# A first layer by seven products for eight, and head pairs mixed with weight conversion, in an attention and gated-FFN kernel

One core of a Trainium2 chip. The metric is device time in microseconds (us), median of several runs; "faster" and "slower" mean by more than 2%.

## The reference

Linear attention without a softmax on 8 batches x 8 heads x 576 tokens x 64, an RMS norm per head, then a gated FFN on 4608 tokens; all float32, except that the three weight matrices arrive as float64.

```python
kv  = einsum('bhsd,bhse->bhde', k, v)
out = einsum('bhsd,bhde->bhse', q, kv)
x   = out / sqrt(mean(out * out, -1) + 1e-6) * g_norm      # (B,H,S,D) -> (B*S, H*D) = (4608, 512)
gate = 1 / (1 + exp(-(x @ w_gate)))                        # w_gate, w_val: (512, 1536)
return (gate * (x @ w_val)) @ w_out                        # w_out: (1536, 512)
```

## The kernel before

It works on nine chunks of 512 tokens. The first layer is one accumulation of four 128x128 by 128x512 matmuls for the gate and four for the value, for each of 12 tiles of 128 features. The weights come in as 64-bit words and are turned into float32 by bit operations, 36 tiles in all (24 for the first layer, then 12 `wo`): GpSimd and ScalarE limit the high word, VectorE does five instructions, GpSimd the last add. Attention of a batch is 16 steps (four for each of 4 head pairs), put one at a time between matmul groups of the chunk ahead. The code is shortened; `...` marks what is left out.

```python
def convert(u):                                  # one weight tile
    ...
    vec.scalar_tensor_tensor(out=yf, in0=a, scalar=HI_MIN, in1=xf, op0=ALU.is_ge, op1=ALU.mult)
    vec.tensor_scalar(out=z, in0=y, ..., op0=ALU.bitwise_and, op1=ALU.logical_shift_left)      # "first mask"
    vec.scalar_tensor_tensor(out=y, in0=y, scalar=0xC0000000, in1=z, ...)
    vec.tensor_scalar(out=z, in0=y, scalar1=0xFF800000, scalar2=None, op0=ALU.bitwise_and)
    vec.scalar_tensor_tensor(out=zf, in0=lo, scalar=2.0 ** -52, in1=zf, op0=ALU.mult, op1=ALU.mult)
    limit(u + 1)
    nc.gpsimd.tensor_tensor(out=flat, in0=zf, in1=yf, op=ALU.add)
    ...

def in_step(c, f):                               # first layer, chunk c, features f
    pg, pv = mm_ps(), mm_ps()
    for ps, name in ((pg, "wg"), (pv, "wv")):
        for m in range(NMT):                     # 4
            nc.tensor.matmul(ps, w[name, f][:, m, :], xT[c][:, m, :], start=(m == 0), stop=(m == NMT - 1))
    nc.scalar.activation(out=sg, in_=pg, func=AF.Sigmoid)
    nc.vector.tensor_tensor(out=gv[c, f], in0=pv, in1=sg, op=ALU.mult)

limit(0)
for step in attention(0): step()                 # batch 0 whole, then conversion begins
convert(0); convert(1)
...
for i, (c, step) in enumerate(todo):             # first layers of chunks 0 and 1, both second layers, then chunk by chunk
    ...
    if ahead: ahead.pop(0)()                     # one attention step of the next batch
    while done < min(2 * i + 4, 2 * NFT) or ...: # about two tiles to a feature step
        convert(done); done += 1
    step()
```

## Time and profile before

| | before |
|---|---|
| time, median (lowest to highest) | 1302.28 us (1301.61 to 1303.0) |
| profiled span | 1298.5 us |
| first attention ends / chunk 1 begins | 54.5 us / 182 us |
| steady chunk with attention / without | 137.2 us / 123.6 us |

The views behind these rows are shown in the prediction. Two more groups by shape matter later (columns: line, engine, operation, output from inputs, shapes, count, busy us, mean ns, idle us before and what ended it): the first mask of the conversion, and the transposes behind the normalising product.

```profile
L122 DVE TENSOR_SCALAR cz<-cy 128x512 uint32<-128x512 uint32 x36 | 27.8, 771 | 1.2
L216 PE MATMUL at<-ident,xn 96*128 96x96 f32 x192 | 23.3, 261 | 20.7 <-DVE xn L208 20.7
```

In the whole kernel TensorE waits 20.7 us for normalising products, all of it in the first attention and in the flush before 182 us (attention steps that are left over and run by themselves).

### The profile page before, as it was taken

The numbers are of one execution on the slowest core, as the hardware profiler recorded it, in microseconds if no ns is written. First come the engines' busy times: TensorE is split into PE (matmuls) and PEld (weight loads), VectorE is DVE, ScalarE is ACT, GpSimd is POOL, SyncE is SP. The second block draws the span as 40 slices with busy tenths as digits, with TensorE's granted clock in tenths as the row PEclk, the third lists the DMA queues.
The fourth block names the chain that finished last, engine by engine and source line by source line (L and its number), as shares of the span: only waits on it lengthen the run. The fifth ranks groups of instructions, "written<-read, shape, count | busy, mean of one in ns | idle before, by whom it ended". The sixth has DMA issues, their size and how long they took to land.

```text
span 1298.5 us, 10116 instructions
## 1 busy us (share of the span) xinstructions
PE 1242.4 (96%) x4128; PEld 599.2 (46%) x4128; DVE 292.8 (23%) x451; ACT 254.2 (20%) x417; POOL 108.1 (8%) x114
## 2 busy tenths in 40 slices
PE   4688879999999999999999999999999999999998
PEld 3443344444444544444444444444444444444443
DVE  1699955520001110111011101110111001000100
ACT  2323332321012211221122112211122110000000
POOL 1366623300000000000000000000000000000000
PEclk8699989999999999999999999999999999999999
DMA  8254423200021102111111011110200000000000
GB/s 188 76 153 138 133 78 117 77 18 25 24 63 28 28 17 62 28 28 26 44 46 28 18 43 37 29 27 24 63 1 1 25 9 0 1 24 9 1 8 25
DMA packets 62350, 57.29 MB, mean 44 GB/s; under 512 B 40800, under 2 KB 53088, under 8 KB 62304
## 3 DMA queue, kind: packets, MB, share of 16 engines
q1 hardware_dynamic: 56960, 37.76, 11.5%
q0 software_dynamic: 5184, 18.88, 4.5%
q8 instruction: 33, 0.54, 0.2%
q14 instruction: 13, 0.11, 0.0%
q10 hardware_dynamic: 160, 0.00, 0.0%
HBM read 47.19 MB, written 9.44 MB: 44 GB/s over the span
## 4 chain that ended last, share of the span: by engine, by line
PE 88%; DVE 8%; issue 1%; DMA 1%; ACT 1%; SPq 0%; POOL 0%; DVEq 0%; ACTq 0%
PE mm L244 52%; PE mm L264 29%; PE at L197 3%; DVE cy L123 2%; PE at L176 2%; DVE cz L122 2%; DVE cy L120 2%; PE at L216 1%; DVE cz L125 1%; PE at L187 1%; DMA v<-in_v_dram 1%; DVE xn L208 1%; DVE gv L248 1%; DVE ms L204 0%; DMA q<-in_q_dram 0%
## 5 line engine op out<-in xcount | busy, mean ns | idle before, releaser
L244 PE MATMUL mm<-xT,wg 128*128 128x512 f32 x864 | 395.5, 601 | 11.4 <-POOL wg L130 11.4
L244 PE MATMUL mm<-xT,wv 128*128 128x512 f32 x864 | 389.5, 593 | 5.9 <-POOL wv L130 5.9
L264 PE MATMUL mm<-wo,gv 128*128 128x512 f32 x864 | 375.4, 592 | 0.0
L244 PEld LDWEIGHTS mm<-xT,wv 128*128 128x128 f32 x864 | 163.2, 190 | 216.4 <-issue 197.8
L264 PEld LDWEIGHTS mm<-wo,gv 128*128 128x128 f32 x864 | 162.3, 190 | 195.2 <-issue 195.2
L244 PEld LDWEIGHTS mm<-xT,wg 128*128 128x128 f32 x864 | 158.4, 191 | 182.9 <-issue 167.7
L248 DVE TENSOR_TENSOR gv<-mm,sg 128x512 f32<-128x512 f32 x108 | 74.6, 691 | 611.2 <-PE mm L244 611.1
L246 ACT ACTIVATE sg<-mm 128x512 f32<-128x512 f32 x108 | 64.4, 596 | 352.2 <-PE mm L244 352.0
L266 ACT COPY out<-mm 128x512 f32<-128x512 f32 x36 | 21.1, 586 | 330.9 <-PE mm L264 275.2
L204 DVE TENSOR_REDUCE ms<-sq 96x12 f32<-96x768 f32 x32 | 30.3, 948 | 168.6 <-ACT sq L203 168.6
L197 PEld LDWEIGHTS at<-kv,qT 128*96 128x96 f32 x384 | 50.5, 180 | 14.6 <-issue 13.6
L197 PE MATMUL at<-kv,qT 128*96 128x128 f32 x384 | 53.2, 294 | 0.3 <-ACT xT L224 0.3
L180 DVE COPY kv<-at 64x64 f32<-64x64 f32 x64 | 14.2, 221 | 153.7 <-PE at L176 151.7
L203 ACT ACTIVATE sq<-at 96x768 f32<-96x768 f32 x32 | 25.8, 807 | 94.0 <-PE at L197 94.0
L224 ACT ACTIVATE xT<-at,g_col 128x288 f32<-128x288 f32 (+8 forms) x96 | 33.5, 421 | 54.5 <-PE at L216 54.5
L216 PE MATMUL at<-ident,xn 96*128 96x96 f32 x192 | 23.3, 261 | 20.7 <-DVE xn L208 20.7
L108 ACT ACTIVATE ca<-st 128x512 f32<-128x512 f32 x36 | 24.5, 680 | 94.6 <-DVE cy L120 46.3
L106 POOL TENSOR_SCALAR cx<-st 128x512 f32<-128x512 f32 x36 | 32.6, 906 | 95.6 <-DVE cy L120 88.7
L176 PEld LDWEIGHTS at<-v,k 96*64 96x64 f32 x768 | 27.6, 149 | 27.1 <-issue 24.7
L176 PE MATMUL at<-v,k 96*64 96x64 f32 x768 | 32.1, 238 | 6.3 <-DMA v<-in_v_dram 6.3
L123 DVE SCALAR_TENSOR_TENSOR cy<-cy,cz 128x512 uint32<-128x512 uint32 x36 | 37.1, 1031 | 1.2
L189 ACT COPY qT<-at 128x576 f32<-128x576 f32 x32 | 20.4, 638 | 86.4 <-PE at L187 86.4
(27 smaller groups left out, 350.1 us busy)
## 6 DMA issues: line engine op xcount, KB each, us to landing
k<-in_k_dram SPq DMA_DIRECT2D x32, 288.0 KB, 3.3
v<-in_v_dram SPq DMA_DIRECT2D x32, 288.0 KB, 3.8
q<-in_q_dram SPq DMA_DIRECT2D x64, 144.0 KB, 3.0
st<-in_moe_w_gate_dram POOLq DMA_DIRECT2D x12, 512.0 KB, 4.0
st<-in_moe_w_val_dram POOLq DMA_DIRECT2D x12, 512.0 KB, 4.3
st<-in_moe_w_out_dram POOLq DMA_DIRECT2D x12, 512.0 KB, 3.6
out_dram<-out SPq DMA_DIRECT2D x24, 192.0 KB, 2.3
out_dram<-out SPq DMA_DIRECT2D x24, 128.0 KB, 2.4
```

The lines of the kernel that those rows point to most:

```text
L106: nc.gpsimd.tensor_scalar(out=x.bitcast(FP32), in0=hi.bitcast(FP32), scalar1=HI_MAX, scalar2=-HI_MAX, op0=ALU.min, op1=ALU.max)
L120: vec.scalar_tensor_tensor(out=yf, in0=a, scalar=HI_MIN, in1=xf, op0=ALU.is_ge, op1=ALU.mult)
L123: vec.scalar_tensor_tensor(out=y, in0=y, scalar=0xC0000000, in1=z, op0=ALU.bitwise_and, op1=ALU.bitwise_or)
L176: nc.tensor.matmul(ps[HD * e:HD * e + HD, 0, 0:HD], kin[:, e, js], vin[:, e, js], start=(j == 0), stop=(j == NJ - 1))
L197: nc.tensor.matmul(ps[0:NP, j // JH, c0:c0 + P], qT[m][:, j // JH, NP * (j % JH):NP * (j % JH) + NP], kvs[m % 2], start=True, stop=True)
L204: nc.vector.tensor_reduce(out=ms.rearrange("p i n -> p (i n)"), in_=sq.rearrange("p i (n d) -> p (i n) d", d=HD), axis=AX.X, op=ALU.add)
L216: nc.tensor.transpose(ps[:, j // JH, c0:c0 + NP], xn[m][:, j // JH, P * (j % JH):P * (j % JH) + P], ident[0:NP, 0:NP])
L224: nc.scalar.activation(out=chunk(c)[:, m, o:o + n], in_=ps[:, i, r:r + n], func=AF.Copy, scale=g_col)
L244: nc.tensor.matmul(ps, w[name, f][:, m, :], xT[c][:, m, :], start=(m == 0), stop=(m == NMT - 1))
L246: nc.scalar.activation(out=sg, in_=pg, func=AF.Sigmoid)
L248: nc.vector.tensor_tensor(out=gv[c, f], in0=pv, in1=sg, op=ALU.mult)
L264: nc.tensor.matmul(ps, gv[c, f][:, P * t:P * t + P], w["wo", f], start=(f == 0), stop=(f == NFT - 1))
```

## The change

Its intent: fewer multiplications in the first layer, and a start in which conversion runs beside the first attention. For chunks 1 to 8 the two matrices (gate, value) and the two halves of the tokens and of the contraction form a 2x2 block product, done in Strassen's way (in the Winograd form) with seven products of 256 columns in place of eight. VectorE makes four sums of x per chunk, GpSimd four sums of weights per feature tile, and the products are added up as they leave the accumulators. Attention becomes 11 fine steps per head pair, taken one to a "slot" between products. Conversion becomes three stages per tile: 20 of the 108 stages go among the first attention, six go behind each feature of chunk 0, and the last 16 go one to a slot in the first half of chunk 1.

```diff
+    with tc.tile_pool(name="psum0", bufs=4, space=bass.MemoryType.PSUM) as psum0:
+        steps = [attention(n, ...) for n in range(NHP)]
+        for t in range(NHP + 2):
+            ...                                   # kv, q of pair t; x of pair t - 2
+            if 0 <= uu < NHP:
+                steps[uu][4](); steps[uu][5]()    # q x kv, square
+                convert_some(2)
+                steps[uu][6](); steps[uu][7]()    # sum, root
+            convert_some(2)
+            if 0 <= uu < NHP:
+                steps[uu][8]()                    # normalising product
...
+    def slot():
+        if fill: fill.popleft()()                 # one attention step
+        if slow: slow.popleft()()                 # one conversion stage (chunk 1, first half)
+    def first_layer(c):                           # chunk 0, plain
+        for f in range(NFT):
+            converted(2 * f + 1)
+            ... the eight matmuls, a slot() after each second one ...
+            nc.vector.tensor_tensor(out=gv_tile(c, f), in0=pv, in1=sg, op=ALU.mult)
+            convert_some(6)
...
+    def w_sum(f, i):                              # four per feature tile
+        nc.gpsimd.tensor_tensor(out=tw[f, i], in0=..., in1=..., op=ALU.subtract)      # 128x256
...
+            def product(ps, wt, xs, new):
+                for m in range(NK):               # 2
+                    nc.tensor.matmul(ps, wt[:, m, :], xs[:, m, :], ...)                # 256 columns
+            def p6():
+                product(pb, tw[f, 2], s[:, 1], True)
+                tt(out=d["h"][:, h1], in0=pb, in1=d["p1"], op=ALU.add)
+            ...                                   # p1, p2, p7, p5, p4, p3 likewise
+            def end(): tt(out=d["h"], in0=d["h"], in1=d["sg"], op=ALU.mult)
...
+    first_layer(0)
+    flush()
+    slow.extend(converts)
+    feed(2)
+    first_layer_fast(1, 0, NFT // 2)
+    while slow: slow.popleft()()
+    second_layer(0)
+    first_layer_fast(1, NFT // 2, NFT)
```

More of the change, by code (lines that the diff above doesn't have):

```diff
@@ L1 @@
 import struct
+from collections import deque
 from contextlib import ExitStack
@@ L43 @@
     NP = S // NJ
+    JH = NJ // 2
     NMT = DM // P
@@ L46, with load_kv @@
     G = 512
+    GH = G // 2
     NG = T // G
-    NLD = 2
     NST = 3
     const = ctx.enter_context(tc.tile_pool(name="const", bufs=1))
-    ld = ctx.enter_context(tc.tile_pool(name="ld", bufs=NLD))
     sb = ctx.enter_context(tc.tile_pool(name="sb", bufs=2))
-    psum = ctx.enter_context(tc.tile_pool(name="psum", bufs=2, space=bass.MemoryType.PSUM))
     ctx.enter_context(tc.manual_schedule())
     pairs = {}
-    def load_pair(n):
+    def load_kv(n):
         if n >= B * NHP:
@@ L63, in load_pair, with load_q @@
         b, h0 = n // NHP, 2 * (n % NHP)
-        pairs[n] = []
+        pairs[n] = {}
         for name, src in (("k", k), ("v", v)):
-            t = ld.tile([NP, 2, NJ * HD], FP32, tag=name, name=name)
+            t = sb.tile([NP, 2, NJ * HD], FP32, tag=name, name=name)
             nc.sync.dma_start(out=t, in_=src[b, h0:h0 + 2].rearrange("h (p j) d -> p h (j d)", j=NJ))
-            pairs[n].append(t)
-        t = ld.tile([NP, NJ, 2, HD], FP32, tag="q", name="q")
+            pairs[n][name] = t
+    def load_q(n):
+        if n >= B * NHP:
+            return
+        b, h0 = n // NHP, 2 * (n % NHP)
+        t = sb.tile([NP, NJ, 2, HD], FP32, tag="q", name="q")
         for e in range(2):
             nc.sync.dma_start(out=t[:, :, e, :], in_=q[b, h0 + e].rearrange("(p j) d -> p j d", j=NJ))
-        pairs[n].append(t)
+        pairs[n]["q"] = t
     units = []
@@ L102, in limit @@
         lo, hi = words(u)
-        x = sb.tile([P, UW], U32, tag="cx", name="cx", bufs=1)
-        a = sb.tile([P, UW], FP32, tag="ca", name="ca", bufs=1)
+        x = sb.tile([P, UW], U32, tag="cx", name="cx")
+        z = sb.tile([P, UW], U32, tag="cz", name="cz")
         nc.gpsimd.tensor_scalar(out=x.bitcast(FP32), in0=hi.bitcast(FP32), scalar1=HI_MAX, scalar2=-HI_MAX,
                                 op0=ALU.min, op1=ALU.max)
-        nc.scalar.activation(out=a, in_=hi.bitcast(FP32), func=AF.Abs)
@@ L109, in limit @@
-        ranged[u] = x, a
+        nc.scalar.activation(out=z.bitcast(FP32), in_=hi.bitcast(FP32), func=AF.Abs)
+        ranged[u] = x, z
     def convert(u):
         name, f, src, shape = units[u]
-        lo, hi = words(u)
-        x, a = ranged.pop(u)
-        y = sb.tile([P, UW], U32, tag="cy", name="cy")
-        z = sb.tile([P, UW], U32, tag="cz", name="cz")
-        xf, yf, zf = x.bitcast(FP32), y.bitcast(FP32), z.bitcast(FP32)
-        vec = nc.vector
-        vec.scalar_tensor_tensor(out=yf, in0=a, scalar=HI_MIN, in1=xf, op0=ALU.is_ge, op1=ALU.mult)
@@ L122, in convert @@
-        vec.tensor_scalar(out=z, in0=y, scalar1=0x07FFFFFF, scalar2=3, op0=ALU.bitwise_and, op1=ALU.logical_shift_left)
-        vec.scalar_tensor_tensor(out=y, in0=y, scalar=0xC0000000, in1=z, op0=ALU.bitwise_and, op1=ALU.bitwise_or)
-        vec.tensor_scalar(out=z, in0=y, scalar1=0xFF800000, scalar2=None, op0=ALU.bitwise_and)
-        vec.scalar_tensor_tensor(out=zf, in0=lo, scalar=2.0 ** -52, in1=zf, op0=ALU.mult, op1=ALU.mult)
-        limit(u + 1)
-        t = const.tile(shape, FP32, name=f"{name}{f}")
@@ L129, in convert, with fl, s0 @@
-        flat = t.rearrange("p m f -> p (m f)") if len(shape) == 3 else t
-        nc.gpsimd.tensor_tensor(out=flat, in0=zf, in1=yf, op=ALU.add)
-        w[name, f] = t
-        load_unit(u + NST)
-    load_pair(0)
-    for u in range(NST):
-        load_unit(u)
-    for n in range(1, NLD):
-        load_pair(n)
+        vec = nc.vector
+        def fl(t):
+            return t.bitcast(FP32)
+        def s0():
+            x, z = ranged[u]
+            vec.scalar_tensor_tensor(out=fl(x), in0=fl(z), scalar=HI_MIN, in1=fl(x), op0=ALU.is_ge, op1=ALU.mult)
@@ new lines, in s1, with s2 @@
+        def s1():
+            x, z = ranged[u]
+            vec.tensor_scalar(out=z, in0=x, scalar1=0x07FFFFFF, scalar2=3, op0=ALU.bitwise_and,
+                              op1=ALU.logical_shift_left)
+            vec.scalar_tensor_tensor(out=x, in0=x, scalar=0xC0000000, in1=z, op0=ALU.bitwise_and, op1=ALU.bitwise_or)
+        def s2():
+            x, z = ranged[u]
+            vec.tensor_scalar(out=z, in0=x, scalar1=0xFF800000, scalar2=None, op0=ALU.bitwise_and)
+            vec.scalar_tensor_tensor(out=fl(z), in0=words(u)[0], scalar=2.0 ** -52, in1=fl(z),
+                                     op0=ALU.mult, op1=ALU.mult)
+            limit(u + 1)
+            t = const.tile(shape, FP32, name=f"{name}{f}")
+            flat = t.rearrange("p m f -> p (m f)") if len(shape) == 3 else t
+            nc.gpsimd.tensor_tensor(out=flat, in0=fl(z), in1=fl(x), op=ALU.add)
+            w[name, f] = t
+            load_unit(u + NST)
@@ L141, with convert_some, converted @@
+        return [s0, s1, s2]
+    converts = deque(s for u in range(len(units)) for s in convert(u))
+    made = [0]
+    def convert_some(n):
+        for _ in range(min(n, len(converts))):
+            converts.popleft()()
+            made[0] += 1
+    def converted(u):
+        convert_some(3 * (u + 1) - made[0])
+    load_kv(0)
+    load_q(0)
+    load_unit(0)
+    load_kv(1)
+    load_q(1)
+    load_unit(1)
+    load_unit(2)
     ident = const.tile([P, P], FP32, name="ident")
@@ L159, in chunk, with attention, kv_mm @@
         return xT[c]
-    def at_ps():
-        return psum.tile([P, 2, 512], FP32, tag="at", name="at")
-    JH = NJ // 2
-    def attention(b):
-        qT, xn = {}, {}
-        def kv_step(m):
-            kin, vin, _ = pairs[NHP * b + m]
-            kv = kvs[m % 2]
-            ps = at_ps()
+    def attention(n, at_ps):
+        b, m = divmod(n, NHP)
+        d = {}
+        def kv_mm():
+            d["kv"] = ps = at_ps()
             for j in range(NJ):
@@ L175, in kv_step, with kv_out @@
                 for e in range(2):
-                    nc.tensor.matmul(ps[HD * e:HD * e + HD, 0, 0:HD], kin[:, e, js], vin[:, e, js],
+                    nc.tensor.matmul(ps[HD * e:HD * e + HD, 0, 0:HD], pairs[n]["k"][:, e, js], pairs[n]["v"][:, e, js],
                                      start=(j == 0), stop=(j == NJ - 1))
+        def kv_out():
             for e in range(2):
                 es = slice(HD * e, HD * e + HD)
-                nc.vector.tensor_copy(out=kv[es, es], in_=ps[es, 0, 0:HD])
@@ L182, in q_step, with q_mm @@
-        def q_step(m):
-            qin = pairs[NHP * b + m][2]
-            ps = at_ps()
+                nc.vector.tensor_copy(out=kvs[n % 2][es, es], in_=d["kv"][es, 0, 0:HD])
+            load_kv(n + 2)
+        def q_mm():
+            d["q"] = ps = at_ps()
             for j in range(NJ):
                 c0 = NP * (j % JH)
-                nc.tensor.transpose(ps[:, j // JH, c0:c0 + NP], qin[:, j].rearrange("p e d -> p (e d)"), ident[0:NP, 0:NP])
-            qT[m] = sb.tile([P, 2, JH * NP], FP32, tag="qT", name="qT")
-            nc.scalar.copy(out=qT[m], in_=ps[:, :, 0:JH * NP])
-            load_pair(NHP * b + m + NLD)
@@ L192, in u_step, with q_out, u_mm @@
-        def u_step(m):
+                nc.tensor.transpose(ps[:, j // JH, c0:c0 + NP], pairs[n]["q"][:, j].rearrange("p e d -> p (e d)"),
+                                    ident[0:NP, 0:NP])
+        def q_out():
+            d["qT"] = sb.tile([P, 2, JH * NP], FP32, tag="qT", name="qT")
+            nc.scalar.copy(out=d["qT"], in_=d["q"][:, :, 0:JH * NP])
+            load_q(n + 2)
+        def u_mm():
             ps = at_ps()
+            d["u"] = ps[0:NP, :, 0:JH * P]
             for j in range(NJ):
@@ L196, in u_step @@
                 c0 = P * (j % JH)
-                nc.tensor.matmul(ps[0:NP, j // JH, c0:c0 + P], qT[m][:, j // JH, NP * (j % JH):NP * (j % JH) + NP],
-                                 kvs[m % 2], start=True, stop=True)
-            u = ps[0:NP, :, 0:JH * P]
-            sq = sb.tile([NP, 2, JH * P], FP32, tag="sq", name="sq", bufs=1)
-            ms = sb.tile([NP, 2, 2 * JH], FP32, tag="ms", name="ms")
-            xn[m] = sb.tile([NP, 2, JH * P], FP32, tag="xn", name="xn", bufs=1)
-            nc.scalar.activation(out=sq, in_=u, func=AF.Square)
@@ L204, in u_step @@
-            nc.vector.tensor_reduce(out=ms.rearrange("p i n -> p (i n)"),
-                                    in_=sq.rearrange("p i (n d) -> p (i n) d", d=HD), axis=AX.X, op=ALU.add)
-            nc.scalar.activation(out=ms, in_=ms, func=AF.Sqrt, bias=eps[0:NP], scale=1.0 / HD)
-            nc.vector.reciprocal(ms, ms)
-            nc.vector.tensor_tensor(out=xn[m].rearrange("p i (n d) -> p i n d", d=HD),
-                                    in0=u.rearrange("p i (n d) -> p i n d", d=HD),
-                                    in1=ms.unsqueeze(3).to_broadcast([NP, 2, 2 * JH, HD]), op=ALU.mult)
@@ L212, in x_step, with u_square, u_sum @@
-        def x_step(m):
-            ps = at_ps()
+                nc.tensor.matmul(ps[0:NP, j // JH, c0:c0 + P], d["qT"][:, j // JH, NP * (j % JH):NP * (j % JH) + NP],
+                                 kvs[n % 2], start=True, stop=True)
+        def u_square():
+            d["sq"] = sb.tile([NP, 2, JH * P], FP32, tag="sq", name="sq", bufs=1)
+            nc.scalar.activation(out=d["sq"], in_=d["u"], func=AF.Square)
+        def u_sum():
+            d["ms"] = sb.tile([NP, 2, 2 * JH], FP32, tag="ms", name="ms")
+            nc.vector.tensor_reduce(out=d["ms"].rearrange("p i n -> p (i n)"),
+                                    in_=d["sq"].rearrange("p i (n d) -> p (i n) d", d=HD), axis=AX.X, op=ALU.add)
@@ new lines, in u_root, with u_norm @@
+        def u_root():
+            nc.scalar.activation(out=d["ms"], in_=d["ms"], func=AF.Sqrt, bias=eps[0:NP], scale=1.0 / HD)
+        def u_norm():
+            nc.vector.reciprocal(d["ms"], d["ms"])
+            d["xn"] = d["sq"]
+            nc.vector.tensor_tensor(out=d["xn"].rearrange("p i (n d) -> p i n d", d=HD),
+                                    in0=d["u"].rearrange("p i (n d) -> p i n d", d=HD),
+                                    in1=d["ms"].unsqueeze(3).to_broadcast([NP, 2, 2 * JH, HD]), op=ALU.mult)
@@ L214, in x_step, with x_mm, x_out @@
+        def x_mm():
+            d["x"] = ps = at_ps()
             for j in range(NJ):
                 c0 = NP * (j % JH)
-                nc.tensor.transpose(ps[:, j // JH, c0:c0 + NP], xn[m][:, j // JH, P * (j % JH):P * (j % JH) + P],
+                nc.tensor.transpose(ps[:, j // JH, c0:c0 + NP], d["xn"][:, j // JH, P * (j % JH):P * (j % JH) + P],
                                     ident[0:NP, 0:NP])
+        def x_out():
             s0 = 0
@@ L222, in x_step @@
                 i, r = divmod(s0, S // 2)
-                n = min(G - o, S // 2 - r)
-                nc.scalar.activation(out=chunk(c)[:, m, o:o + n], in_=ps[:, i, r:r + n], func=AF.Copy, scale=g_col)
-                s0 += n
-        steps = []
-        for t in range(NHP + 2):
-            for step, m in ((kv_step, t), (x_step, t - 2), (q_step, t), (u_step, t - 1)):
-                if 0 <= m < NHP:
-                    steps.append(lambda step=step, m=m: step(m))
-        return steps
-    gv = {}
@@ L237, in mm_ps @@
-    def mm_ps():
-        return psum.tile([P, 512], FP32, tag="mm", name="mm", bufs=4)
-    def in_step(c, f):
-        pg, pv = mm_ps(), mm_ps()
-        for ps, name in ((pg, "wg"), (pv, "wv")):
-            for m in range(NMT):
-                nc.tensor.matmul(ps, w[name, f][:, m, :], xT[c][:, m, :], start=(m == 0), stop=(m == NMT - 1))
-        sg = sb.tile([P, G], FP32, tag="sg", name="sg")
-        nc.scalar.activation(out=sg, in_=pg, func=AF.Sigmoid)
-        gv[c, f] = sb.tile([P, G], FP32, tag="gv", name="gv", bufs=2 * NFT)
-        nc.vector.tensor_tensor(out=gv[c, f], in0=pv, in1=sg, op=ALU.mult)
+                n_ = min(G - o, S // 2 - r)
@@ new lines, in x_out @@
+                nc.scalar.activation(out=chunk(c)[:, m, o:o + n_], in_=d["x"][:, i, r:r + n_], func=AF.Copy, scale=g_col)
+                s0 += n_
+        return [kv_mm, kv_out, q_mm, q_out, u_mm, u_square, u_sum, u_root, u_norm, x_mm, x_out]
+    limit(0)
+    with tc.tile_pool(name="psum0", bufs=4, space=bass.MemoryType.PSUM) as psum0:
+        steps = [attention(n, lambda: psum0.tile([P, 2, 512], FP32, tag="at", name="at")) for n in range(NHP)]
+        for t in range(NHP + 2):
+            kv, qq, uu, xx = t, t, t - 1, t - 2
+            if kv < NHP:
+                for i in range(4):
+                    steps[kv][i]()
+            if 0 <= xx < NHP:
+                steps[xx][9]()
+                steps[xx][10]()
+            if 0 <= uu < NHP:
+                steps[uu][4]()
+                steps[uu][5]()
+                convert_some(2)
+                steps[uu][6]()
+                steps[uu][7]()
+            convert_some(2)
+            if 0 <= uu < NHP:
+                steps[uu][8]()
@@ new lines, with feed, mm_ps @@
+    psum = ctx.enter_context(tc.tile_pool(name="psum", bufs=1, space=bass.MemoryType.PSUM))
+    fill = deque()
+    slow = deque()
+    def slot():
+        if fill:
+            fill.popleft()()
+        if slow:
+            slow.popleft()()
+    def feed(b):
+        for n in range(NHP * b, NHP * b + NHP):
+            fill.extend(attention(n, lambda: psum.tile([P, 2, 512], FP32, tag="at", name="at")))
+    def mm_ps():
+        return psum.tile([P, 512], FP32, tag="mm", name="mm", bufs=6)
@@ new lines, with gv_tile, sg_tile @@
+    gv = {}
+    def gv_tile(c, f):
+        gv[c, f] = sb.tile([P, G], FP32, tag="gv", name="gv", bufs=NFT + NFT // 2)
+        return gv[c, f]
+    def sg_tile():
+        return sb.tile([P, G], FP32, tag="sg", name="sg", bufs=3)
+    def first_layer(c):
+        for f in range(NFT):
+            converted(2 * f + 1)
+            pg, pv = mm_ps(), mm_ps()
+            for ps, name in ((pg, "wg"), (pv, "wv")):
+                for m in range(NMT):
+                    nc.tensor.matmul(ps, w[name, f][:, m, :], xT[c][:, m, :], start=(m == 0), stop=(m == NMT - 1))
+                    if m % 2:
+                        slot()
+                if name == "wg":
+                    sg = sg_tile()
+                    nc.scalar.activation(out=sg, in_=pg, func=AF.Sigmoid)
+            nc.vector.tensor_tensor(out=gv_tile(c, f), in0=pv, in1=sg, op=ALU.mult)
+            convert_some(6)
@@ new lines, with x_sums @@
+    NK = NMT // 2
+    sx, tw = {}, {}
+    def x_sums(c):
+        x = xT[c]
+        a = {(i, j): x[:, NK * (j - 1):NK * j, GH * (i - 1):GH * i] for i in (1, 2) for j in (1, 2)}
+        sx[c] = s = sb.tile([P, 4, NK, GH], FP32, tag="sx", name="sx", bufs=1)
+        tt = nc.vector.tensor_tensor
+        return [
+            lambda: tt(out=s[:, 0], in0=a[2, 1], in1=a[2, 2], op=ALU.add),
+            lambda: tt(out=s[:, 1], in0=s[:, 0], in1=a[1, 1], op=ALU.subtract),
+            lambda: tt(out=s[:, 2], in0=a[1, 1], in1=a[2, 1], op=ALU.subtract),
+            lambda: tt(out=s[:, 3], in0=a[1, 2], in1=s[:, 1], op=ALU.subtract),
+        ]
@@ new lines, in w_sum, with first_layer_fast, block, p1 @@
+    def w_sum(f, i):
+        b = {(j, n): w[name, f][:, NK * (j - 1):NK * j, :] for n, name in ((1, "wg"), (2, "wv")) for j in (1, 2)}
+        tw[f, i] = sb.tile([P, NK, P], FP32, tag=f"tw{i}", name=f"tw{i}")
+        in0, in1 = {1: ((1, 2), (1, 1)), 2: ((2, 2), 1), 3: ((2, 2), (1, 2)), 4: ((2, 1), 2)}[i]
+        nc.gpsimd.tensor_tensor(out=tw[f, i], in0=b[in0], in1=b[in1] if isinstance(in1, tuple) else tw[f, in1],
+                                op=ALU.subtract)
+    def first_layer_fast(c, f0=0, f1=NFT):
+        x, s = xT[c], sx[c]
+        a = {(i, j): x[:, NK * (j - 1):NK * j, GH * (i - 1):GH * i] for i in (1, 2) for j in (1, 2)}
+        h1, h2 = slice(0, GH), slice(GH, G)
+        tt = nc.vector.tensor_tensor
+        def block(f):
+            d = {}
+            pa, pb, pc = (mm_ps()[:, h1] for _ in range(3))
+            bg, bv = w["wg", f], w["wv", f]
+            def product(ps, wt, xs, new):
+                for m in range(NK):
+                    nc.tensor.matmul(ps, wt[:, m, :], xs[:, m, :], start=(new and m == 0), stop=(m == NK - 1),
+                                     skip_group_check=True)
+            def p1():
+                product(pa, bg[:, 0:NK], a[1, 1], True)
+                d["p1"] = sb.tile([P, GH], FP32, tag="p1", name="p1")
+                nc.scalar.copy(out=d["p1"], in_=pa)
+            def p6():
+                product(pb, tw[f, 2], s[:, 1], True)
+                d["h"] = gv_tile(c, f)
+                tt(out=d["h"][:, h1], in0=pb, in1=d["p1"], op=ALU.add)
+            def p2():
+                product(pa, bg[:, NK:], a[1, 2], False)
+                d["sg"] = sg_tile()
+                nc.scalar.activation(out=d["sg"][:, h1], in_=pa, func=AF.Sigmoid)
+            def p7():
+                product(pb, tw[f, 3], s[:, 2], False)
+                tt(out=d["h"][:, h2], in0=pb, in1=d["p1"], op=ALU.add)
+            def p5():
+                product(pc, tw[f, 1], s[:, 0], True)
+                tt(out=d["h"][:, h2], in0=pc, in1=d["h"][:, h2], op=ALU.add)
+            def p4():
+                product(pb, tw[f, 4], a[2, 2], False)
+                tt(out=d["sg"][:, h2], in0=pb, in1=d["p1"], op=ALU.add)
+                nc.scalar.activation(out=d["sg"][:, h2], in_=d["sg"][:, h2], func=AF.Sigmoid)
+            def p3():
+                product(pc, bv[:, NK:], s[:, 3], False)
+                tt(out=d["h"][:, h1], in0=pc, in1=d["h"][:, h1], op=ALU.add)
+            def end():
+                tt(out=d["h"], in0=d["h"], in1=d["sg"], op=ALU.mult)
+            return [p1, p6, p2, p7, p5, p4, p3], end
+        for n, i in ((0, 1), (0, 2), (1, 1), (1, 2), (0, 3), (1, 3), (0, 4), (1, 4)):
+            w_sum(f0 + n, i)
+        for f in range(f0, f1, 2):
+            one, two = block(f), block(f + 1)
+            for i, (p, r) in enumerate(zip(one[0], two[0])):
+                p()
+                r()
+                slot()
+                if f + 2 < f1:
+                    for n, k_ in {4: ((0, 1), (1, 1), (0, 2), (1, 2), (0, 3), (1, 3)), 5: ((0, 4), (1, 4))}.get(i, ()):
+                        w_sum(f + 2 + n, k_)
+            one[1]()
+            two[1]()
@@ L259, in store @@
             r0 += n
-    def out_step(c, t):
-        ps = mm_ps()
-        for f in range(NFT):
-            nc.tensor.matmul(ps, gv[c, f][:, P * t:P * t + P], w["wo", f], start=(f == 0), stop=(f == NFT - 1))
-        ot = sb.tile([P, DM], FP32, tag="out", name="out")
-        nc.scalar.copy(out=ot, in_=ps)
-        store(c, t, ot)
-    def ffn_in(c):
-        return [lambda f=f: in_step(c, f) for f in range(NFT)]
-    def ffn_out(c):
-        return [lambda t=t: out_step(c, t) for t in range(G // P)]
@@ L276 @@
-    limit(0)
-    for step in attention(0):
-        step()
-    convert(0)
-    convert(1)
-    done = 2
-    ahead = []
-    fed = 1
-    todo = [(0, s) for s in ffn_in(0)] + [(1, s) for s in ffn_in(1)] + [(1, s) for s in ffn_out(0) + ffn_out(1)]
-    for c in range(2, NG):
-        todo += [(c, s) for s in ffn_in(c) + ffn_out(c)]
-    last = -1
-    for i, (c, step) in enumerate(todo):
-        if c != last:
-            for a in ahead:
-                a()
-            ahead = attention(fed) if fed < B and fed <= c + 1 else []
-            fed += bool(ahead)
-            last = c
-        if ahead:
-            ahead.pop(0)()
-        while done < min(2 * i + 4, 2 * NFT) or i >= NFT and done < min(NFT + i + 2, len(units)):
-            convert(done)
-            done += 1
-        step()
@@ L301, with second_layer, flush, sums @@
-    assert fed == B and not ahead
+    def second_layer(c):
+        for t in range(G // P):
+            ps = mm_ps()
+            for f in range(NFT):
+                nc.tensor.matmul(ps, gv[c, f][:, P * t:P * t + P], w["wo", f], start=(f == 0), stop=(f == NFT - 1))
+                if f % 2:
+                    slot()
+            ot = sg_tile()
+            nc.scalar.copy(out=ot, in_=ps)
+            store(c, t, ot)
+    def flush():
+        while fill:
+            fill.popleft()()
+    def sums(c):
+        if c < NG:
+            fill.append(lambda: fill.extendleft(reversed(x_sums(c))))
@@ L305 @@
+    feed(1)
+    sums(1)
+    first_layer(0)
+    flush()
+    slow.extend(converts)
+    converts.clear()
+    feed(2)
+    first_layer_fast(1, 0, NFT // 2)
+    while slow:
+        slow.popleft()()
+    second_layer(0)
+    first_layer_fast(1, NFT // 2, NFT)
+    sums(2)
+    second_layer(1)
+    flush()
+    for c in range(2, NG):
+        if c + 1 < B:
+            feed(c + 1)
+        first_layer_fast(c)
+        sums(c + 1)
+        second_layer(c)
+        flush()
 _INS = ['q', 'k', 'v', 'g_norm', 'moe_w_gate', 'moe_w_val', 'moe_w_out']
```

## The prediction

> **What bounds the kernel now.** I read the page first: shares of busy time, the slices, the chain that ended last.
>
> ```profile
> PE 1242.4 (96%) x4128; PEld 599.2 (46%) x4128; DVE 292.8 (23%) x451; ACT 254.2 (20%) x417; POOL 108.1 (8%) x114
> ...
> PE   4688879999999999999999999999999999999998
> ...
> DVE  1699955520001110111011101110111001000100
> ...
> PEclk8699989999999999999999999999999999999999
> ...
> PE 88%; DVE 8%; issue 1%; DMA 1%; ACT 1%; SPq 0%; POOL 0%; DVEq 0%; ACTq 0%
> ```
>
> TensorE is the bound from about slice 7 (some 190 us) to the end; before that it has holes while VectorE is full. VectorE's 8% of the chain lies there. Next the groups by shape, and the chain in order of time at its end, where no attention is left:
>
> ```profile
> L244 PE MATMUL mm<-xT,wg 128*128 128x512 f32 x864 | 395.5, 601 | 11.4 <-POOL wg L130 11.4
> L244 PEld LDWEIGHTS mm<-xT,wg 128*128 128x128 f32 x864 | 158.4, 191 | 182.9 <-issue 167.7 <-POOL wg L130 13.5
> ```
> ```profile
> 1046.72 82.40 PE mm L244 x192
> 1129.12 41.20 PE mm L264 x96
> ```
>
> A float32 matmul of the program is two instructions in the trace (9 chunks x 12 x 4 = 432 for the gate weights, 864 recorded). The mean of 601 ns is a latency; the rate is in the chain: 82.40 us / 192 = 429.2 ns per 512-column instruction. A chunk of 512 tokens is 82.4 us of first layer and 41.2 of second, 123.6 us with no hole. Then a table of stretches, one for each stage (columns: length, then busy us and count of PE, PEld, DVE, ACT, POOL, then granted clock, DMA share and GB/s):
>
> ```profile
> 0.00:54.50 54.50, 25.70 (x216) 22.91 (x216) 15.31 (x30) 15.53 (x29) 6.30 (x13) 0.75 0.56 132
> 54.50:164.00 109.50, 94.38 (x317) 42.58 (x317) 104.29 (x139) 33.74 (x53) 71.53 (x71) 0.99 0.46 140
> 164.00:182.00 18.00, 10.40 (x68) 7.67 (x68) 4.95 (x7) 5.59 (x11) 0.46 (x1) 0.86 0.09 30
> 182.00:275.00 93.00, 93.00 (x334) 45.16 (x332) 54.24 (x86) 27.88 (x42) 29.78 (x32) 0.99 0.30 89
> ...
> 635.80:773.00 137.20, 137.20 (x482) 66.45 (x480) 18.58 (x32) 28.16 (x47) 0.00 (x0) 1.00 0.13 34
> ```
>
> The first batch's attention ends at 54.5; chunk 0 runs to 164 at the pace of VectorE's weight conversion (104 of 109.5 us busy); the rest of batch 1's attention is flushed by itself to 182; from there on TensorE has no hole. A steady chunk with attention takes 137.2 us, 13.6 more than without. VectorE's pace, from its timeline, is two converted weight tiles, one gv product and one pair of kv copies in 9.2 us:
>
> ```profile
> 139.38 0.68 DVE L120 SCALAR_TENSOR_TENSOR cy<-ca,cx 128x512 f32<-128x512 f32 x1
> ...
> 148.59 0.69 DVE L120 SCALAR_TENSOR_TENSOR cy<-ca,cx 128x512 f32<-128x512 f32 x1
> ```
>
> Less 0.7 for gv and 0.5 for the copies, that is 4.0 us per weight tile.
>
> **What the Trainium skill says.** (1) "TensorE: Matmul & The Clock Gate", section "Back-to-back issue gap": the isolated warm gap is N/2.4 + 2.5 ns. Taken twice over 512 columns plus 2.5 once this gives 429.2 ns, what the trace has; so one instruction here is two passes (four for a float32 product, as "FP8 and Floating Point Precision", section "TensorE Precision Notes", has it), and 256 columns should take 213.3 + 2.5 = 215.8 ns, an estimate. (2) The same page, step 1 of "Step-by-step: what each phase is for": the next weights load while the current matmul runs. The trace agrees at 512 columns (no hole with a 190 ns load in each 429 ns); at 256 the load has 215.8. (3) "SBUF — State Buffer", section "SBUF: two separate sides": VectorE instructions with two SBUF inputs and GpSimd share a port pair as an exclusive lock. The trace fits: the first mask of the conversion takes 0.43 or 1.38 us, the latter while GpSimd adds.
>
> **The change, part by part.** *First layer.* Chunk 0 stays plain. In chunks 1 to 8 each tile of 128 features needs 7 products x 2 halves of the contraction x 2 instructions = 28 instructions of 256 columns, in place of 16 of 512. Per chunk 12 x 28 = 336 x 215.8 ns = 72.5 us for 192 x 429.2 = 82.4: 9.9 us saved, all on the path, 8 x 9.9 = 79 us.
>
> *What it adds beside that.* For two features, one round of 14 products: 12.1 us of TensorE without attention. VectorE: ten additions of 128x256 with a PSUM operand. The 128x512 gv product takes 691 ns and the 64x64 copy out of PSUM 221 (groups by shape), so about 1.05 ns a column and 221 + 192 x 1.05 = 0.42 us for 256; with two final products of about 0.65, 5.5 us. GpSimd: eight sums of 128x256; the add of 128x512 took 1.27 us undisturbed, so half and a little, some 0.68 each, 5.4 us. ScalarE: six instructions of about 0.4. All below 12.1 us. Each accumulator is read two products (1.7 us) or more before the next product writes it, so these lie beside TensorE. The exception is attention: the normalising product (0.95 us after a 0.22 us reciprocal) stands behind two additions, and the transposes that need it come one slot (1.7 us) later: 0.4 + 1.2 + about 0.3 of latencies is 0.2 us over. Four pairs a chunk, and kv copies and table loads (1.28 us each) now and then: 1 to 1.5 us per chunk with attention, 6 us in all.
>
> *First attention.* Twenty of the 108 conversion stages (6.7 tiles) move in among it. A turn of its loop took 8.8 us (24.5 to 33.4 in the timeline). Two stages (2.7 us) now stand before the normalising product, of which 1 us or so was waiting for the root anyway: about 10 us a turn, four turns. The end goes from 54.5 to about 58. Gain later: 4.7 tiles fewer to convert, 19 us of VectorE.
>
> *Chunk 0.* All of batch 1's attention is now inside its 48 slots, where the kernel before left a third for 164 to 182. VectorE per feature: 8.0 (two tiles) + 0.7 + 0.9 (attention) = 9.6 us; TensorE 6.9 + 1.2 = 8.1. So VectorE lags. The six stages of a feature are one block of 8 us in its order; kv copies and normalising products stand behind that block, and TensorE, which takes its attention steps in order, waits for them. I walked the twelve features by hand with these numbers: TensorE stops 3 to 8 us at the transposes of each pair, and VectorE then waits for that feature's matmuls, some 14 us in all. Chunk 0 takes 12 x 9.6 + 14 = 129, ends near 188, with restarts at a low clock near 190: 8 us later than the 182 of before.
>
> *Opening of chunk 1.* VectorE is then still at its last six stages until about 201, and GpSimd's weight sums stand in its order behind the add of the last of these tiles. The second product needs them: TensorE waits about 13 us. In the three rounds that follow, 16 stages come one to a slot: VectorE has 5.5 + 7 x 1.4 + 1.7 = 17 us a round, TensorE 14.3, so some 6 us more. In the kernel before, these conversions lay hidden beside chunk 1.
>
> Sum: 1302 - 79 + 8 + 19 + 6 = 1256.
>
> **Rivals.** *A. The start costs nothing.* The mixing hides as meant and ends chunk 0 some 8 us early: 1302 - 79 - 8 + 6 = 1221. For it: less conversion is left after the first attention, and there are six accumulators in place of four. Against it: in-order VectorE blocks of 8 us with attention behind them. *B. VectorE and GpSimd block each other at the start more than I reckon* (the adds, the limits and the weight sums share the port), 20 us worse: 1276. *C. The weight load binds at 256 columns.* If the pitch is 190 ns of load plus a hand-over of 50, 2688 x 24 ns = 65 us go and 1320 is left. Against it, in the timeline of a steady chunk, 12 instructions of 128 columns with 96-column loads, recorded at 180 ns each on average:
>
> ```profile
> 727.20 1.47 PE L197 MATMUL at<-kv,qT 128*96 128x128 f32 x12
> 727.20 1.25 PEld L197 LDWEIGHTS at<-kv,qT 128*96 128x96 f32 x11 [0.27 <-issue]
> ```
>
> That is 122 ns a matmul: most of a load's recorded time is latency that overlaps. *D. The steady rounds stall on VectorE, ScalarE or GpSimd*, 5 us a chunk: 1275. Against it, the loads above are all under half of the round.
>
> **Range and chances.** Between A (1221) and B or D (1275) I put the middle at 1256; the saving of 79 us is arithmetic on a measured pitch, the start is not. 8 in 10: 1230 to 1282. Faster by over 2% means below 1276: 0.87; within 2%: 0.12; slower: 0.01 (only C).
>
> **What would show it.** Right: in the last two chunks 336 instructions of 256 columns in about 72.5 us, with no hole; steady chunks with attention of 127 to 129 us; first 512-column matmul at about 58; the 256-column ones from about 190, with a hole of 10 us or so on GpSimd's sums or VectorE; VectorE over 85% busy up to there. Wrong: a pitch above 225 ns (C), steady chunks above 131 us (D), or 256-column matmuls that begin before 180 (A) or after 200 (B).

## The result

1271.42 us (1271.16 to 1271.57, 4 runs) against 1302.64 us of the kernel before: ratio 0.976, 95% interval 0.9743 to 0.9777, faster. The output is right. A ratio here is the mean time of one kernel's fast runs over that of the other's fast runs of the same rounds, so not quite the ratio of the quoted medians.

The page of the kernel after (shares, slices of 31.7 us, granted clock, chain):

```profile
PE 1174.5 (93%) x5280; PEld 822.3 (65%) x5280; DVE 532.2 (42%) x963; ACT 319.9 (25%) x621; POOL 391.2 (31%) x498
...
PE   4477775799999999999999999999999999999998
...
DVE  3667998951422542154215421542054305513530
...
PEclk9688897899999999999999999999999999999999
...
PE 81%; DVE 10%; issue 2%; ACT 1%; POOL 1%; DVEq 0%; ACTq 0%
```

TensorE's holes now last to slice 8, where before they ended in slice 6, and its clock is lower there. Behind slice 8 the profile is full. The chain at its end, and the groups of the new matmuls, their weight loads and the conversion's first mask:

```profile
1037.34 72.52 PE mm L372 x336
1109.86 41.20 PE mm L443 x96
```
```profile
L372 PE MATMUL mm<-sx,tw 128*128 128x256 f32 x1152 | 270.8, 384 | 13.1 <-POOL tw L355 13.1
L372 PEld LDWEIGHTS mm<-sx,tw 128*128 128x128 f32 x1152 | 217.7, 192 | 42.7 <-POOL tw L355 13.9
L131 DVE TENSOR_SCALAR cz<-cx 128x512 uint32<-128x512 uint32 x36 | 45.7, 1271 | 1.0
```

72.52 / 336 = 215.8 ns an instruction, with no hole. By stages (length, then busy us and count of PE, PEld, DVE, ACT, POOL, then clock, DMA share, GB/s), first attention, chunk 0, first half of chunk 1's first layer, one steady chunk:

```profile
0.00:58.40 58.40, 24.18 (x192) 21.86 (x193) 30.52 (x56) 17.53 (x33) 21.89 (x29) 0.81 0.69 166
58.40:200.30 141.90, 109.94 (x384) 54.04 (x385) 108.82 (x140) 42.81 (x67) 68.79 (x64) 0.86 0.35 105
200.30:269.30 69.00, 47.70 (x266) 40.27 (x264) 62.07 (x90) 20.42 (x38) 44.89 (x53) 0.85 0.24 73
...
523.40:651.90 128.50, 127.95 (x626) 93.61 (x625) 45.09 (x96) 37.06 (x72) 33.95 (x48) 1.00 0.14 37
```

The steady chunk is 128.5 us for 137.2. Chunk 0 takes 141.9 us, and in it neither TensorE (109.9 us busy) nor VectorE (108.8) is full. TensorE's timeline has the stops of chunk 0 and of the opening of chunk 1 in brackets, two of them and the largest at the opening:

```profile
90.49 1.19 PE L253 MATMUL at<-ident,sq 96*128 96x96 f32 x6 [9.29 <-DVE sq L245]
...
106.51 1.22 PE L213 MATMUL at<-ident,q 96*128 96x96 f32 x6 [5.45 <-DVE kv L206]
...
216.20 4.07 PE L372 MATMUL mm<-sx,tw 128*128 128x256 f32 x8 [13.13 <-POOL tw L355]
```

So a transpose waits for a normalising product or a pair of kv copies, and the second product of chunk 1 waits for a weight sum. The same two waits in the table of who waited for whom, over the whole kernel (total us, times, longest), and VectorE's wait for the matmuls of chunk 0, which is most of its 33 us of idle time there:

```profile
PE at L253 <- DVE sq L245: 55.1, 14, 9.3
...
PE mm L372 <- POOL tw L355: 13.1, 1, 13.1
DVE gv L330 <- PE mm L324: 23.4, 4, 6.8
```

### The profile page after: what moved, and what is told of

It reads as the page before. It is cut to its first block, busy times and chain, and to the rows that moved or that the text cites. A ratio compares the mean times of both kernels' runs of the same rounds, so it can differ in the third digit from the quotient of the medians.

```text
span 1269.4 us, 14111 instructions
## 1 busy us (share of the span) xinstructions
PE 1174.5 (93%) x5280; PEld 822.3 (65%) x5280; DVE 532.2 (42%) x963; ACT 319.9 (25%) x621; POOL 391.2 (31%) x498
## 4 chain that ended last, share of the span: by engine, by line
PE 81%; DVE 10%; issue 2%; ACT 1%; POOL 1%; DVEq 0%; ACTq 0%
PE mm L372 44%; PE mm L443 29%; DVE cz L131 3%; PE at L227 2%; DVE cx L133 2%; PE mm L324 2%; PE at L200 2%; DVE cx L126 2%; PE at L253 1%; DVE cz L138 1%; PE at L213 1%; DVE sq L245 1%; POOL tw L355 1%; ACT L240 1%; DVE gv L330 0%
## 5 line engine op out<-in xcount | busy, mean ns | idle before, releaser
L372 PE MATMUL mm<-sx,tw 128*128 128x256 f32 x1152 | 270.8, 384 | 13.1 <-POOL tw L355 13.1
L372 PEld LDWEIGHTS mm<-sx,tw 128*128 128x128 f32 x1152 | 217.7, 192 | 42.7 <-POOL tw L355 13.9
L372 PE MATMUL mm<-xT,wg 128*128 128x256 f32 x768 | 182.6, 381 | 0.0
L384 DVE TENSOR_TENSOR gv<-mm,p 128x256 f32<-128x256 f32 x96 | 40.6, 424 | 333.0 <-PE mm L372 333.0
L393 DVE TENSOR_TENSOR gv<-mm,p 128x256 f32<-128x256 f32 x96 | 40.7, 425 | 124.0 <-PE mm L372 124.0
L372 PE MATMUL mm<-xT,tw 128*128 128x256 f32 x384 | 91.4, 381 | 0.0
L372 PE MATMUL mm<-sx,wv 128*128 128x256 f32 x384 | 91.2, 380 | 0.0
L409 DVE TENSOR_TENSOR gv<-gv,sg 128x512 f32<-128x512 f32 x96 | 79.8, 871 | 0.2
L372 PEld LDWEIGHTS mm<-sx,wv 128*128 128x128 f32 x384 | 72.2, 190 | 9.7
L372 PEld LDWEIGHTS mm<-xT,tw 128*128 128x128 f32 x384 | 72.0, 190 | 9.7
L355 POOL TENSOR_TENSOR tw<-wg,tw 128x256 f32<-128x256 f32 x96 | 77.8, 830 | 0.0
```

The lines of the kernel that those rows point to most:

```text
L355: nc.gpsimd.tensor_tensor(out=tw[f, i], in0=b[in0], in1=b[in1] if isinstance(in1, tuple) else tw[f, in1], op=ALU.subtract)
L372: nc.tensor.matmul(ps, wt[:, m, :], xs[:, m, :], start=(new and m == 0), stop=(m == NK - 1), skip_group_check=True)
L384: tt(out=d["h"][:, h1], in0=pb, in1=d["p1"], op=ALU.add)
L393: tt(out=d["h"][:, h2], in0=pb, in1=d["p1"], op=ALU.add)
L409: tt(out=d["h"], in0=d["h"], in1=d["sg"], op=ALU.mult)
```

## The experiments

**The theory.** The product scheme pays in full. The start loses, because VectorE's stages come in blocks of six behind gv, attention's VectorE steps wait behind the block, TensorE waits for them, and then VectorE waits for TensorE's gv. **Rivals:** the scheme pays less than its arithmetic and the start is neutral; the lock on the port that VectorE and GpSimd share makes conversion dearer and VectorE is just full; the 13 us hole is GpSimd's order alone; the mixing buys nothing.

### One part of the change at a time

The start of the change with the plain first layer everywhere:

```diff
-        first_layer_fast(c)
-        sums(c + 1)
+        first_layer(c)          # and both halves of chunk 1, without conversion calls for c > 0
```

> The change's schedule for the start (conversion mixed into the first attention, head pairs in slots), but the plain first layer with 512-column matmuls in every chunk; right results. Theory (the product scheme pays its 79 us in full, the new start costs some 35 to 45 us): 79 us come back to 1271, less the 13 us hole at the weight sums and a part of the stall behind it, which go with the scheme: 1320 to 1335, slower than before. Rival (the start is neutral and the scheme pays only some 31 us): 1302.

Measured: 1330.02 us, ratio 1.0211 (1.0194 to 1.0228): slower than before, though the interval does not clear the 2% line. Inside the range of the theory; the rival's 1302 is out. The change's start alone makes the kernel 28 us slower, and the scheme is worth 59 us with this start: 79, less 6 in the steady chunks and some 14 at the opening of chunk 1 (that half takes 60.2 us in e1 and 69.0 in the change, where the arithmetic alone would save 5).

The start of the kernel before, with the scheme from chunk 2 on (the wo tiles converted a little faster, since a smaller gv buffer puts the second layer of chunk 0 ahead of the last features of chunk 1); the diff is shortened:

```diff
-    first_layer(0); flush(); ...; first_layer_fast(1, ...)
+    # attention in 16 coarse steps, two tiles converted per feature, chunks 0 and 1 plain, as before
     for c in range(2, NG):
         first_layer_fast(c)
```

> The start of the kernel before (order of TensorE, conversion and attention as there, chunks 0 and 1 plain), the product scheme in chunks 2 to 8 only; right results. Theory: chunks 2 to 6 take 128.5 us for 137.2, chunks 7 and 8 113.7 for 123.6, so 5 x 8.7 + 2 x 9.9 = 63 us off 1302: 1239, and faster than the change although chunk 1 has not got the scheme. Rival (the scheme itself loses something that the start hides): above 1255.

Measured: 1239.66 us, ratio 0.9518 (0.9504 to 0.9532), 32 us faster than the change with one chunk less by the scheme. The chain has the last chunks as in the kernel after:

```profile
1006.37 72.52 PE mm L352 x336
```

So the scheme does not lose anything that the start hides. The 63 us reckoned for seven chunks are there.

### Why the start loses

The stages of chunk 0 spread over the slots, nothing else changed:

```diff
                     if m % 2:
                         slot()
+                        convert_some(1 + (m == 1))
...
-            convert_some(6)
```

> The change, but in chunk 0 the six conversion stages of a feature are spread over its four slots (2, 1, 2, 1) in place of one block behind its gv product; the same work on each engine. Theory (attention's VectorE steps wait behind a block of 8 us, TensorE waits for them, VectorE then for TensorE): the waits for the normalising product and the kv copies in chunk 0 shrink from about 32 us to under 15, chunk 0 from 142 us to 120 to 128: 1250 to 1257. Rival (the port lock makes each tile 0.45 us dearer, 24 tiles, and VectorE is simply full): first mask still at 1.3 us on average and the time within 5 us of 1271.

Measured: 1237.58 us, ratio 0.9503 (0.9489 to 0.9518), 34 us faster than the change, more than the 14 to 21 expected. Its stages, and its waits for the normalising products and the kv copies in chunk 0 alone (25.1 and 6.0 us there in the change):

```profile
58.30:174.40 116.10, 103.91 (x384) 50.58 (x385) 108.43 (x147) 45.14 (x69) 72.20 (x69) 0.94 0.44 133
174.40:234.40 60.00, 47.94 (x265) 40.51 (x264) 53.38 (x83) 19.32 (x36) 39.52 (x48) 0.89 0.25 74
```
```profile
PE at L253 <- DVE sq L245: 10.8, 4, 3.9
PE at L213 <- DVE kv L206: 1.4, 2, 1.0
```

In chunk 0 VectorE is busy for the same 108 us in 116.1 us as it was in 141.9: its idle time fell from 33 us to 8. Order alone did that. The rival of a full VectorE is out. The two waits fell from 31 us to 12, as expected (under 15). What the expectation missed is that chunk 0 became even shorter (116 us, not 120 to 128) and ends with less left over: VectorE got 147 instructions done in it for 140, and the next stage is 60.0 us for 69.0. The first mask fell too, from 1271 to 1065 ns on average.

GpSimd's first weight sums issued earlier, behind feature 8 of chunk 0:

```diff
             convert_some(6)
+            if f == 8:
+                for n, i in (...): w_sum(n, i)
...
-            w_sum(f0 + n, i)
+            if (c, f0) != (1, 0):
+                w_sum(f0 + n, i)
```

> The change, but GpSimd's eight weight sums for the first two features of chunk 1 are issued behind feature 8 of chunk 0, ahead of the last conversions. Theory (the 13 us hole is GpSimd's order): the hole at the second product goes, but VectorE is still at its last six stages, so TensorE stops one or two products later and most comes back: 1263 to 1269. If GpSimd's order alone were the cause: 1258.

Measured: 1272.24 us, ratio 0.9771 (0.9756 to 0.9786): no gain, 3 us slower than even the theory's range. The hole at the second product is gone, and three others stand in its place, all behind VectorE or ScalarE:

```profile
208.38 2.58 PE L375 MATMUL mm<-sx,tw 128*128 128x256 f32 x8 [2.11 <-DVE sx L349]
213.23 3.55 PE L375 MATMUL mm<-xT,wg 128*128 128x256 f32 x8 [2.27 <-ACT p L381]
221.43 1.22 PE L213 MATMUL at<-ident,q 96*128 96x96 f32 x6 [4.65 <-DVE kv L206]
```

The hole was labelled GpSimd, but the arrears were VectorE's. The opening half itself is 1.8 us shorter (67.2 us for 69.0), but chunk 0, into which the sums were moved, ends 3.2 us later (its wait for the last normalising product was 10.7 us).

The last add of a tile on VectorE, so that GpSimd's add cannot hold the port:

```diff
-            nc.gpsimd.tensor_tensor(out=flat, in0=fl(z), in1=fl(x), op=ALU.add)
+            vec.tensor_tensor(out=flat, in0=fl(z), in1=fl(x), op=ALU.add)
```

> The change, but the last add of each converted weight tile runs on VectorE and not on GpSimd; same results. If the first mask takes 1.27 us on average because GpSimd's add holds the shared port, it falls to 0.43 to 0.6 us, a tile costs VectorE some 4.1 us with its add in place of 4.5 without, and GpSimd's weight sums come earlier: 1255 to 1265. Rival (the length of the mask has another cause, and a sixth instruction is just more work for the full engine): 24 x 0.7 us more, 1280 to 1290.

Measured: 1265.81 us, ratio 0.972 (0.9704 to 0.9736), 6 us faster than the change. The first mask in the groups by shape:

```profile
L131 DVE TENSOR_SCALAR cz<-cx 128x512 uint32<-128x512 uint32 x36 | 26.6, 740 | 1.0
```

It fell from 1271 to 740 ns, not to the 430 to 600 expected (GpSimd still limits and sums). Taking GpSimd's add away shortens a VectorE instruction that does not read its result, so the two do hold each other up. The 6 us are a net gain: over the kernel the first masks take 19 us less of VectorE and the instruction behind them (L133) 11 us less, but VectorE now has 26 us of adds. What the hold-ups cost in all is not separated.

### Does the mixing into the first attention pay?

The change without conversion stages there:

```diff
                 steps[uu][4](); steps[uu][5]()
-                convert_some(2)
...
-            convert_some(2)
             if 0 <= uu < NHP:
```

> The change, but no conversion stage among the first batch's attention (the two calls left out); the first tiles are then converted in front of chunk 0. Theory (the mixing lengthens the first attention by 4 us and takes 6.7 tiles, 27 us of VectorE, off the crowded stages behind it): first matmul of chunk 0 at about 62 as against 58, end of chunk 0 near 205, and 14 more stages in the first half of chunk 1 or before the second layer: 1283 to 1293. Rival (the mixing buys nothing, the loss lies in the blocks alone): 1268 to 1274.

Measured: 1314.3 us, ratio 1.0094 (1.0079 to 1.0109). A miss for both expectations: 43 us slower than the change, where 12 to 22 were expected. First matmul of chunk 0 at 51.4 us, not 62; chunk 0 ends at 234 us, not 205. TensorE's timeline repeats one stop per feature, two of them here:

```profile
84.00 6.17 PE L322 MATMUL mm<-xT,wg 128*128 128x512 f32 x8 [5.96 <-POOL wg L144]
...
99.67 5.16 PE L322 MATMUL mm<-xT,wg 128*128 128x512 f32 x8 [4.70 <-POOL wg L144]
```

With no tile in stock, a feature's matmuls wait for the block of six stages, and the block stands behind the gv product of the feature before, which waits for its matmuls: the engines take turns, about 15.2 us a feature (183 us for twelve). So inside the change the mixing is worth 43 us, but as a stock that keeps the two apart, not as VectorE time saved.

Two steps towards a better start came next. First, stages spread and features 0 to 5 of chunk 1 by the plain form:

```diff
     # as e3_spread, and
-    first_layer_fast(1, 0, NFT // 2)
+    first_layer(1, 0, NFT // 2)      # no conversion calls of its own for c = 1
```

> Stages spread over the slots of chunk 0 as in e3_spread, and in addition features 0 to 5 of chunk 1 by the plain first layer, so that no product sums stand beside the last 16 conversion stages. Theory (these six features take 60 us in e3_spread by the product scheme, as VectorE has 17 us a round and GpSimd starves it; plain they need 6 x 6.9 + 7 = 48 to 51 us): 1226 to 1230, although the plain form has 5 us more of matmuls. Rival (the stall there comes from attention and conversion alone): 1240 to 1243.

Measured: 1229.47 us, ratio 0.9446 (0.9431 to 0.9461), 8 us faster than e3_spread, at the upper end of the theory's range. Beside the last conversions the scheme costs more than it saves. The edit takes away both GpSimd's sums and VectorE's additions of the scheme, so it does not tell which of the two mattered. The timeline of the change shows one reason. First GpSimd (eight sums and a limit, merged in twos), then VectorE at the same time:

```profile
229.20 1.42 POOL L355 TENSOR_TENSOR tw<-wv,wg 128x256 f32<-128x256 f32 x2
230.58 1.41 POOL L355 TENSOR_TENSOR tw<-wv,tw 128x256 f32<-128x256 f32 x2
231.95 1.41 POOL L355 TENSOR_TENSOR tw<-wv 128x256 f32<-128x256 f32 x2
233.32 1.41 POOL L355 TENSOR_TENSOR tw<-wg,tw 128x256 f32<-128x256 f32 x2
234.71 0.66 POOL L111 TENSOR_SCALAR cx<-st 128x512 f32<-128x512 f32 x1
```
```profile
229.78 5.87 DVE L131 TENSOR_SCALAR cz<-cx 128x512 uint32<-128x512 uint32 x1
```

A mask that takes 0.43 us undisturbed lasts 5.87 us, until GpSimd's row of instructions ends at 235.4. The normalising product behind it comes late, and TensorE's stop of 8.2 us at 244 us is for that product.

Then the add on VectorE as well:

```diff
     # as e8_spread_half_plain, with the edit of e5_add_on_vector
```

> As e8_spread_half_plain, with the last add of each tile on VectorE. In e3_spread a tile costs VectorE 4.05 us and its gaps; with the add and without the lock it would be about 4.0 too. Theory: within 6 us of e8_spread_half_plain. If the lock costs more than the one first mask shows (other VectorE instructions too): 8 us or more faster than it.

Measured: 1225.68 us, ratio 0.9412 (0.9398 to 0.9426), 4 us faster than e8, as expected.

Last, the same without the mixing, which tells whether the stock still matters when there are no blocks:

```diff
     # as e9_spread_half_plain_add_vector, with the edit of e7_no_mix
```

> As e9_spread_half_plain_add_vector, but no conversion stage among the first attention, as in e7_no_mix. In e7_no_mix chunk 0 took 188 us, as each feature's matmuls and the block of six stages for the next feature took turns. Theory (the mixing is needed because the blocks make the engines take turns unless some tiles are ready in advance; with the stages in the slots there are no turns): it costs far less than the 43 us of e7_no_mix, at most 15: 1226 to 1241. Rival (the head start of 6.7 tiles is worth its 27 us of VectorE and more in any order): above 1252.

Measured: 1218.98 us, ratio 0.9372 (0.9356 to 0.9387). Not only less than 15 us lost, but 7 us gained: outside the expected range, on the good side. The first matmuls of chunk 0 in the two kernels, e9 and then e10:

```profile
60.97 3.69 PE L325 MATMUL mm<-xT,wg 128*128 128x512 f32 x4 [1.13 <-ACT xT L263]
```
```profile
48.10 3.75 PE L323 MATMUL mm<-xT,wg 128*128 128x512 f32 x4 [2.51 <-DVE wg L144]
```

The first attention is 13 us shorter, and 5 of these are lost again by the second layer of chunk 0 (216.6 as against 224.2 us). With blocks the mixing was worth 43 us; without them it costs 7. This is the fastest kernel, 6.3% below before and 52 us below the change. The two pairs stand on different bases (e7 with the scheme in all of chunk 1 and GpSimd's add), so the sign is shown, not the exact difference; e3 without the mixing, which would change the blocks alone, was not run.

## Why the prediction was right, and what was mis-sized

| term of the sum | predicted | measured | how read |
|---|---|---|---|
| product scheme, chunks 1 to 8 | -79 | -79.0 | 8 x (82.40 - 72.52) |
| stalls in steady chunks | +6 | +6 | 5 x ((128.5 - 113.7) - (137.2 - 123.6)) |
| first attention and chunk 0 | +8 | +18.3 | 200.3 - 182.0 |
| opening of chunk 1 | +19 | +25.5 | 69.0 - 43.5, the half without stalls (36.3 + 7.2 of attention) |
| sum | -46 | -29 | span 1298.5 to 1269.4 |

- **The bound and the scheme: right.** A 256-column instruction takes 215.8 ns, to the tenth. The weight loads, recorded at 192 ns, make no hole (rival C is out), and e1 and e2 confirm by removal that the scheme pays.
- **The load on the other engines in a steady round: right in what it decides.** The 256-column additions take 424 ns as reckoned; the final product 871 ns on average instead of 650 (676 at the least) and the sums 732 to 830 instead of 680 (715 at the least). TensorE has 127.95 us of 128.5 busy, so rival D is out. The 1.2 us a chunk lies where the prediction had it: in the chunk that begins at 523 us, the transposes behind the normalising products start about 0.2, 0.2, 0 and 0.6 us later than the pitch of the products gives.
- **First attention: right,** 58.4 us for 58.
- **Chunk 0: the right mechanism, the wrong size.** The walk by hand gave 12 x 9.6 + 14: VectorE's work 115 us, its idle time 14. The trace has 108.8 us of work and 33 us idle. The mis-sized term is the 14 us of turn-taking; the work was even less than reckoned. The sign that I named for it, VectorE over 85% busy, was wrong (108.8 / 141.9 = 77%) and would have said so at once. The walk allowed 2 us in all for restarts at a low clock (188 to 190), but the clock in this stage is 0.86, and the eight instructions (half a feature) behind a stop of 9.3 us took 5.1 us in place of 3.6; this lengthens VectorE's next wait too. How much of the 19 us the clock has is not separated. That order is the cause and not the amount of work is shown by e3: same work, 26 us less. (The kernel before leaves 4 of 16 attention steps to the flush, a quarter and not the third that I wrote; no term rests on it.)
- **Opening of chunk 1: the hole of 13 us right in size and place, the rest 12 us for 6.** I took VectorE's load from undisturbed durations. The trace has a mask of 5.87 us there, and e8, which takes the scheme's sums and additions away from this stretch, gains 8 us over e3.
- **Rival A (the mixing hides the start) is out; the "gain later, 19 us of VectorE" was the wrong reason.** The mixing pays in this change because it breaks the turns (e7), and costs where there are none (e10). I had the sign right for this change, and would have had it wrong for the spread one.
- **Rival B (port lock)** is there, but its size stays open. The 6 us of e5 are net of the adds that VectorE took over, and the mask of 5.87 us, beside weight sums, looks like the same thing, so a part of the 12 us in the opening may be B's. In chunk 0 it is the smaller part: 138.1 us in e5 for 141.9, where e3 has 116.1. Point (3) named instructions with two SBUF inputs, but the mask that it gave as a witness reads one; the instruction behind it (L133), which reads two, shows the hold-up as well (1047 ns, 733 in e5).
- **The total:** both mis-sized terms erred to the same side, and the range was wide enough for it. By time alone, 1271 is nearer to B (1276) and D (1275) than to the middle of 1256; only the traces and the experiments tell them apart.

Why the change moves the time by 2.4% and not by the 6% of its arithmetic: 44 of the 79 us are given back before 270 us, some 18 in chunk 0 and 25 in chunk 1, and about 6 in steady chunks. In e10 all of it is had again and more: 83 us below the kernel before, where the arithmetic of its seven and a half chunks gives 74.

## What to carry to other kernels

A stage in which no engine is full is a question of order: count the idle time of both engines, and look for a block of one engine's instructions that has work for the other behind it. Cut such a block into the slots in which the other engine comes by before adding any overlap; a head start that helps with the blocks can be a loss without them. A wait labelled with one engine may be the arrears of another: moving the labelled instruction earlier (e4) is a cheap test.

## What the Trainium skill lacked or had wrong

- "SBUF — State Buffer", section "Who interferes with whom": it has the exclusive lock held for one instruction, which the first mask agrees with (0.43 us free, 1.38 beside GpSimd's add; the mask reads one SBUF operand, so of that section's cases only the 2-port modes can cover it). It does not say that the waiting engine need not get a turn between two instructions of the other: one VectorE mask took 5.87 us beside nine GpSimd instructions in a row.
- "TensorE: Matmul & The Clock Gate", section "Back-to-back issue gap": its isolated gap fits float32 if each recorded instruction is two passes with one fixed 2.5 ns (429.2 ns at 512 columns, 215.8 at 256), which the page does not say. Its sustained figure of about 131 ns at 512 columns is seen nowhere in these runs, which are streams of load and matmul pairs: a pass over 512 columns takes 214.6 ns (half of 429.2). All of them are float32.
